# A state-space layer and a gated feed-forward on one core: the head without a diagonal, up rows loaded ahead of x tile 2, and its transposes in two banks

## The chip, the cores and the metric

The kernel runs on one core of one Trainium2 chip. The metric is the device time of one launch in microseconds (us); of several runs the median is taken. A core has five engines, each with a queue of its own that it works off in order: TensorE (PE in the profile; PEld is its weight load), VectorE (DVE), ScalarE (ACT), GpSimd (POOL) and SyncE (SP, which here only issues transfers). They wait for each other through semaphores. TensorE writes only to PSUM, which has eight banks of 128 x 512 float32; VectorE and ScalarE copy the results out ("evict" them) to SBUF.

## The reference

Input x is 2048 x 512 in bfloat16. It is normalised by rows, and two branches work on the result:

```python
x = A_x
xn = layernorm(x)                                  # rows of 512
# A: a diagonal complex state-space layer, 512 states
Lam_bar = exp(exp(log_dt) * Lam)
Bu = xn @ B_bar.T
h[t] = Lam_bar * h[t-1] + Bu[t]                    # 2048 steps
A = 2 * real(h @ C.T) + xn * Dskip
# B: a gated feed-forward, 512 -> 1376 -> 512
B = (silu(xn @ w_gate) * (xn @ w_up)) @ w_down
out = x + A + B                                    # bfloat16
```

## The kernel before

The 2048 rows are 16 tiles of 128 rows, in four chunks of four tiles. Every engine's instructions stand in an order written out by hand. Later chunks are normalised, transposed by DMA into xnT and multiplied from there. Chunk 0 has its own way through gate and up, so that TensorE can start before any row is normalised: this is the head, and the change is in it.

**Head, tiles 0 and 1.** The column sum of each row tile is not taken off in SBUF but in PSUM. TensorE transposes the raw tile in four blocks of 128 columns by products with the identity (`raw_mm`, `cT_mm`, L244) and adds a product of the constant minus_mean (all entries -1/512) with a diagonal matrix of the row sums (`cT_mean`, L252). The sums come from VectorE for tile 0 (`sum_dve`, L221) and from ScalarE for tile 1 (`sum_act`, L224); `diag_dve` (L231) makes the diagonals. `cT_copy` (L256) copies each block, centred and transposed, into xcT. Warming products (`dummy`, L646) on a constant go ahead of and between these.

**Head, tiles 2 and 3.** Tile 2 is centred in SBUF with a mean from ScalarE (`mean_act`, L227; `center`, L234), tile 3 with the mean of its statistics. TensorE then transposes the centred tile into one bank (p1 for tile 2, p0 for tile 3) and ScalarE copies it out whole.

**Gate and up of chunk 0.** `head_mm` (`sw_mm`, L488) multiplies the transposed blocks with the first 512 columns of w_gate (which = 0) and w_up (which = 1); their 512 rows come in four row blocks k of 128, as weights wg and wu. Results of tile i stay in the banks held[i][0] and held[i][1] until `sw_out` (L497, L498) evicts them on ScalarE with a factor rstd, the row's inverse deviation. rstd needs statistics (`ln_stats`, L187 and L188, on VectorE), a variance plus eps (`ln_rstd`, L196, VectorE) and a power on GpSimd (L197). After the head two more groups of columns follow in the same way for all four tiles (gi = 1, 2), with new banks: group 1's third gate tile gets the bank that held[2][0] had.

**Beside it.** On GpSimd, behind the rstd powers, `exp_pool` (L284) makes dt_t, then come the memsets of `pad_last`, an iota (L725) and another power. On VectorE, behind the head, come `norm_dve` (L205), which writes the normalised tiles for the transpose by DMA, and the small parameter steps `params_a` and `params_sin` (L287 to L334). The two sines of `params_sin` (L339, L341) stand in ScalarE's queue between sw_out of tile 1 and sw_out of tile 2.

**Loads.** SP's queue loads, in this order: x tile 0, w_gate row blocks 0 and 2, x tile 2, w_up row blocks 0 and 1 together, 2 and 3 together, x tile 3, and the later groups. ScalarE's queue loads x tile 1 and w_gate row blocks 1 and 3.

Of the kernel before, what the change touches and what calls it, by code (L numbers as in the profile page):

```python
# [10 lines left out]
F32 = mybir.dt.float32  # L11
BF16 = mybir.dt.bfloat16
ALU = mybir.AluOpType
ACT = mybir.ActivationFunctionType
# [9 lines left out]
def kernel(  # L24
# [17 lines left out]
    nc = tc.nc  # L42
    _, L, D = A_x.shape
# [4 lines left out]
    HW = CW // 2  # L48
    NT = L // 128
    NCH = L // CW  # L50
    TPC = CW // 128
    KD = D // 128
# [11 lines left out]
    const = ctx.enter_context(tc.tile_pool(name="const", bufs=1))  # L64
# [9 lines left out]
    def bank(shape=(128, CW), dtype=F32):  # L74
        return psum.tile(list(shape), dtype, name="ps")

    def flat(ap3):
        return ap3.rearrange("p q j -> p (q j)")
# [4 lines left out]
    wu_v = B_w_up.rearrange("(k p) f -> p k f", p=128)  # L83


    xall = const.tile([128, NT, D], BF16, name="xall")
    xnT = const.tile([128, NCH, KD, CW], BF16, name="xnT")

    fgroups = [(0, 4), (4, 8), (8, FT - 1)]
    wg_g, wu_g = [], []  # L90
# [26 lines left out]
    def load_w1_half(q, tiles, view, gi, k0, k1):  # L117
        a, b = fgroups[gi]
        q.dma_start(out=tiles[gi][:, k0:k1, :], in_=view[:, k0:k1, a * 128:min(F, b * 128)])

    HK = KD // 2
    ident = const.tile([128, 128], BF16, name="ident")
    make_identity(nc, ident[:])
    minus_mean = const.tile([128, 128], BF16, name="minus_mean")
    nc.sync.dma_start(out=xall[:, 0, :], in_=x_v[:, 0, :])
    nc.vector.memset(xall[:, 1, 0:2], 0.0)
    nc.vector.memset(minus_mean[:], -1.0 / D)
    nc.scalar.dma_start(out=xall[:, 1, :], in_=x_v[:, 1, :])
    nc.scalar.preload_act_table_set("silu_and_others")
    for k in range(KD):  # L130
        load_w1_half(nc.scalar if k % 2 else nc.sync, wg_g, wg_v, 0, k, k + 1)
    nc.sync.dma_start(out=xall[:, 2, :], in_=x_v[:, 2, :])
    load_w1_half(nc.sync, wu_g, wu_v, 0, 0, HK)
    load_w1_half(nc.sync, wu_g, wu_v, 0, HK, KD)
    nc.sync.dma_start(out=xall[:, 3, :], in_=x_v[:, 3, :])
    load_w1(nc.sync, wg_g, wg_v, 1)
# [35 lines left out]
    mv = const.tile([128, NT, 2], F32, name="mv")  # L172
# [10 lines left out]
    def by_k(ap):  # L183
        return ap.rearrange("p (k d) -> p k d", d=128)

    def ln_stats(n):
        nc.vector.bn_stats(out=stats[:, n, 0, :], in_=xall[:, n, :])  # L187
        nc.vector.bn_aggr(out=mv[:, n, :], in_=stats[:, n, 0, :])  # L188

    def ln_stats_half(n, h):  # L190
        nc.vector.bn_stats(out=stats[:, n, h, :], in_=xall[:, n, h * HW:(h + 1) * HW])
        if h == 1:
            nc.vector.bn_aggr(out=mv[:, n, :], in_=stats[:, n, :, :])

    def ln_rstd(a, b):
        nc.vector.tensor_scalar(out=ve[:, a:b], in0=mv[:, a:b, 1], scalar1=EPS, scalar2=None, op0=ALU.add)  # L196
        nc.gpsimd.tensor_tensor(out=rstd[:, a:b], in0=ve[:, a:b], in1=neg_half[:, 0:b - a], op=ALU.pow)  # L197
# [16 lines left out]

    xcT, xc = CF[:, 0], CF[:, 1]
    xn_c[0] = flat(xc).rearrange("p (k i d) -> p k i d", k=KD, i=TPC)
    sums = const.tile([128, 2], F32, name="sums")
    diag = const.tile([128, 2, 128], BF16, name="diag")

    def sum_dve(i):  # L220
        nc.vector.tensor_reduce(out=sums[:, i:i + 1], in_=xall[:, i, :], axis=mybir.AxisListType.X, op=ALU.add)  # L221

    def sum_act(i):
        nc.scalar.activation(out=xnT[:, NCH - 1, 0, :], in_=xall[:, i, :], func=ACT.Copy, accum_out=sums[:, i:i + 1])  # L224

    def mean_act(i):
        nc.scalar.activation(out=xnT[:, NCH - 1, 0, :], in_=xall[:, i, :], func=ACT.Copy, scale=1.0 / D,  # L227
                             accum_out=mean2[:])

    def diag_dve(i):  # L230
        nc.vector.tensor_scalar(out=diag[:, i, :], in0=ident[:], scalar1=sums[:, i:i + 1], scalar2=None, op0=ALU.mult)  # L231

    def center(i, mean):
        nc.vector.tensor_scalar(out=xc[:, i, :], in0=xall[:, i, :], scalar1=mean, scalar2=None, op0=ALU.subtract)  # L234

    mean2 = const.tile([128, 1], F32, name="mean2")
    p2, p0, p1 = bank(), bank(), bank()
    held = [[None, None] for _ in range(TPC)]
    held[0][0], held[1][0], held[0][1], held[1][1], held[2][0] = (bank() for _ in range(5))
    warm = held[1][0]  # L240
    raw = [[p0, p1, held[2][0], held[1][1]], [p2, p2, held[0][1], held[0][1]]]

    def cT_mm(ps, src, k, first, stop):
        nc.tensor.matmul(ps[:, k * 128:(k + 1) * 128], lhsT=src[:, k * 128:(k + 1) * 128], rhs=ident[:], start=first,  # L244
                         stop=stop)

    def raw_mm(i):
        for k in range(KD):
            cT_mm(raw[i][k], xall[:, i, :], k, k == 0 or raw[i][k] is not raw[i][k - 1], False)

    def cT_mean(i, k0, k1):
        nc.tensor.matmul(raw[i][k0][:, k0 * 128:k1 * 128], lhsT=minus_mean[:],  # L252
                         rhs=diag[:, i:i + 1, :].to_broadcast([128, k1 - k0, 128]), start=False, stop=True)

    def cT_copy(copy, ps, i, k0=0, k1=KD):
        copy(out=xcT[:, k0:k1, i * 128:(i + 1) * 128], in_=by_k(ps[:, k0 * 128:k1 * 128]))  # L256

    seen = const.tile([128, 1], BF16, name="seen")

    def runs(ap):  # L260
        return ap.rearrange("p k (i t) -> p (k i) t", t=128)
# [14 lines left out]
    V = nc.vector  # L276
# [208 lines left out]
    def sw_mm(ps, groups, gi, i, k0=0, k1=KD):  # L485
        a, b = fgroups[gi]
        for k in range(k0, k1):
            nc.tensor.matmul(ps[:, 0:(b - a) * 128], lhsT=xcT[:, k, i * 128:(i + 1) * 128], rhs=groups[gi][:, k, 0:(b - a) * 128],  # L488
                             start=(k == 0), stop=(k == KD - 1))
# [154 lines left out]
    def dummy(ps, n, cols):  # L644
        for _ in range(n):
            nc.tensor.matmul(ps[:, 0:cols], lhsT=one.to_broadcast([128, 128]), rhs=one.to_broadcast([128, cols]),  # L646
                             start=True, stop=True)
# [22 lines left out]
    def head_mm(which, i, k0=0, k1=KD):  # L670
        if held[i][which] is None:
            held[i][which] = bank()
        sw_mm(held[i][which], (G, U)[which], 0, i, k0, k1)

    dummy(warm, 4, CW)
    dummy(warm, 5, 128)
    V.tensor_copy(out=seen[:], in_=ident[:, 0:1])
    sum_dve(0)
    sum_act(1)
    diag_dve(0)  # L680
    raw_mm(0)
    raw_mm(1)
    dummy(warm, 2, 128)
    for k in range(KD):
        cT_mean(0, k, k + 1)
    diag_dve(1)
    for k in range(KD):
        cT_copy(nc.scalar.copy if k % 2 else V.tensor_copy, raw[0][k], 0, k, k + 1)
    cT_mean(1, 0, HK)
    head_mm(0, 0, 0, 1)  # L690
    cT_mean(1, HK, KD)
    cT_copy(V.tensor_copy, raw[1][0], 1, 0, HK)
    cT_copy(nc.scalar.copy, raw[1][HK], 1, HK, KD)
    head_mm(0, 0, 1, HK)
    head_mm(0, 1, 0, HK)
    for k in range(HK, KD):
        for i in range(2):
            head_mm(0, i, k, k + 1)
    ln_stats(1)
    mean_act(2)  # L700
    ln_rstd(1, 2)
    ln_stats_half(0, 0)
    center(2, mean2[:])
    ln_stats_half(0, 1)
    ln_rstd(0, 1)
    for i in range(2):
        head_mm(1, i, 0, HK)
    for k in range(KD):
        cT_mm(p1, xc[:, 2, :], k, k == 0, k == KD - 1)
    cT_copy(nc.scalar.copy, p1, 2)  # L710
    for i in range(2):
        head_mm(1, i, HK, KD)
    ln_stats(3)
    center(3, mv[:, 3, 0:1])
    ln_rstd(3, 4)
    ln_stats(2)
    ln_rstd(2, 3)
    head_mm(0, 2)
    for k in range(KD):
        cT_mm(p0, xc[:, 3, :], k, k == 0, k == KD - 1)  # L720
# [158 lines left out]
```

## Time and profile before

| | us |
|---|---|
| median of three runs | 178.81 |
| lowest and highest | 178.35, 178.82 |
| profiled execution, its own time | 178.46 |
| its span, first to last instruction | 176.4 |
| TensorE busy in the span | 172.9 (98%) |
| VectorE busy | 158.1 (90%) |
| ScalarE busy | 106.6 (60%) |
| GpSimd busy | 27.8 (16%) |

The profile is of one execution. Times in the timeline are counted from the start of the span; each line gives start, busy time, engine, line of the kernel, operation, what it writes and reads, the number of instructions, and in brackets the idle time before it and what ended it. Matmuls are pipelined, so the busy time of a group is longer than the distance to the next group's start: the distance between starts tells the pace. The page gives the granted clock of TensorE as full throughout; the rows in the first microseconds are slower than later ones of the same form.

Landings of the loads, from the trace (us): x tile 0 3.20, x tile 1 3.54, w_gate rows 0 to 3 3.91, 4.28, 5.47 and 6.02, x tile 2 6.42, w_up rows 0 and 1 6.94, rows 2 and 3 7.62, x tile 3 8.00.

### The profile page before, as it was taken

The numbers are of one execution on the slowest core, as the hardware profiler recorded it, in microseconds if no ns is written. First come the engines' busy times: TensorE is split into PE (matmuls) and PEld (weight loads), VectorE is DVE, ScalarE is ACT, GpSimd is POOL, SyncE is SP. The second block draws the span as 40 slices with busy tenths as digits, with TensorE's granted clock in tenths as the row PEclk, the third lists the DMA queues.
The fourth block names the chain that finished last, engine by engine and source line by source line (L and its number), as shares of the span: only waits on it lengthen the run. The fifth ranks groups of instructions, "written<-read, shape, count | busy, mean of one in ns | idle before, by whom it ended". The sixth has DMA issues, their size and how long they took to land.

```text
span 176.4 us, 2469 instructions
## 1 busy us (share of the span) xinstructions
PE 172.9 (98%) x904; PEld 85.4 (48%) x904; DVE 158.1 (90%) x261; ACT 106.6 (60%) x192; POOL 27.8 (16%) x39
## 2 busy tenths in 40 slices
PE   8999999999999999999999999999999999999993
PEld 4444755564444444446444444446444444444743
DVE  3899999999999999999999999999999997799133
ACT  4468989978976687036896661024666657962000
POOL 5272300050000000047000000024100002416100
PEclk9999999999999999999999999999999999999999
DMA  6999839999996000037015000007410000993712
GB/s 169 340 351 203 177 88 250 224 169 337 238 238 238 4 0 0 0 33 85 16 20 119 0 0 0 0 4 71 48 30 2 4 0 0 160 181 48 90 44 75
DMA packets 35179, 17.88 MB, mean 101 GB/s; under 512 B 25008, under 2 KB 35088, under 8 KB 35120
## 3 DMA queue, kind: packets, MB, share of 16 engines
q1 hardware_dynamic: 30992, 13.96, 33.8%
q0 software_dynamic: 3456, 3.28, 14.6%
q10 hardware_dynamic: 720, 0.49, 0.9%
q8 instruction: 7, 0.11, 0.3%
q14 instruction: 4, 0.03, 0.1%
HBM read 8.03 MB, written 5.24 MB: 75 GB/s over the span
## 4 chain that ended last, share of the span: by engine, by line
PE 97%; DMA 1%; DVE 0%; issue 0%
PE ps L461 29%; PE ps L579 22%; PE ps L589 16%; PE ps L386 16%; PE ps L488 10%; PE ps L521 3%; DMA xall<-in_A_x_dram 1%; PE ps L244 1%; PE ps L252 0%; DVE xall L592 0%; PE ps L646 0%; PE ps L280 0%
## 5 line engine op out<-in xcount | busy, mean ns | idle before, releaser
L579 PE MATMUL ps<-wd_sb,guT 128*128 128x512 bf16 (+3 forms) x198 | 38.8, 355 | 0.0
L428 DVE TENSOR_TENSOR_SCAN g<-r_t,car,u 128x512 bf16<-128x512 f32 x24 | 29.1, 1264 | 0.0
L589 PE MATMUL ps<-CF,wt 128*128 128x512 bf16 (+2 forms) x144 | 28.3, 355 | 0.0
L386 PE MATMUL ps<-xnT,BT 128*128 128x512 bf16 x128 | 28.3, 379 | 0.0
L579 PEld LDWEIGHTS <-guT 128*128 128x128 bf16 (+1 forms) x198 | 18.5, 98 | 19.9
L461 PE MATMUL ps<-xnT,wg 128*128 128x512 bf16 x96 | 24.6, 379 | 0.0
L461 PE MATMUL ps<-xnT,wu 128*128 128x512 bf16 x96 | 24.6, 379 | 0.0
L596 POOL DMA_DIRECT2D out_dram<-res x12 | 10.5, 1043 | 81.6 <-ACT res L595 76.0
L595 ACT CAST res<-ps 128x512 bf16<-128x512 f32 x12 | 7.0, 584 | 24.7 <-PE ps L589 24.7
L388 ACT CAST u<-ps 128x512 bf16<-128x512 f32 x32 | 18.2, 590 | 5.9 <-PE ps L386 5.8
L475 ACT ACTIVATE guT<-ps 128x512 bf16<-128x512 f32 x30 | 17.9, 596 | 6.1 <-PE ps L461 6.1
L476 ACT CAST u<-ps 128x512 bf16<-128x512 f32 x30 | 17.6, 587 | 6.0 <-PE ps L461 6.0
L589 PEld LDWEIGHTS <-wt 128*128 128x128 bf16 x144 | 13.4, 98 | 14.3
L386 PEld LDWEIGHTS <-BT 128*128 128x128 bf16 x128 | 12.5, 98 | 14.7
L551 ACT ACTIVATE xr<-xall,nb,rstd 128x512 bf16<-128x512 bf16 x16 | 11.8, 804 | 5.2 <-DVE xall L559 3.0
L461 PEld LDWEIGHTS <-wu 128*128 128x128 bf16 x96 | 9.4, 98 | 11.3
L461 PEld LDWEIGHTS <-wg 128*128 128x128 bf16 x96 | 9.4, 98 | 10.6
L488 PEld LDWEIGHTS <-CF 128*128 128x128 bf16 x96 | 9.1, 98 | 8.0 <-ACT CF L256 0.8
L197 POOL TENSOR_TENSOR rstd<-ve,neg_half 128x1 f32<-128x1 f32 (+1 forms) x7 | 7.6, 1084 | 26.7 <-DVE ve L196 26.7
L461 PE MATMUL ps<-xnT,w_end 128*128 128x512 bf16 x48 | 10.8, 379 | 0.0
L187 DVE BATCH_NORM_STATS2 stats<-xall 128x6 f32<-128x512 bf16 x15 | 10.1, 674 | 0.2 <-DMA xall<-in_A_x_dram 0.2
L480 DVE TENSOR_TENSOR guT<-guT,u 128x1024 bf16<-128x1024 bf16 x15 | 10.0, 675 | 0.0
(120 smaller groups left out, 217.9 us busy)
## 6 DMA issues: line engine op xcount, KB each, us to landing
out_dram<-in_A_x_dram SPq DMA_DIRECT2D x3, 512.0 KB, 5.2
out_dram<-res POOLq DMA_DIRECT2D x12, 128.0 KB, 3.1
out_dram<-xall POOLq DMA_DIRECT2D x3, 512.0 KB, 6.1
wd_sb<-in_B_w_down_dram SPq DMA_DIRECT2D x1, 1280.0 KB, 7.2
xall<-in_A_x_dram SPq DMA_DIRECT2D x1, 1024.0 KB, 7.3
wu<-in_B_w_up_dram SPq DMA_DIRECT2D x2, 256.0 KB, 4.4
wg<-in_B_w_gate_dram SPq DMA_DIRECT2D x1, 512.0 KB, 5.3
wu<-in_B_w_up_dram SPq DMA_DIRECT2D x1, 512.0 KB, 5.4
```

The source lines that it names most:

```text
L187: nc.vector.bn_stats(out=stats[:, n, 0, :], in_=xall[:, n, :])
L386: nc.tensor.matmul(ps[:], lhsT=BT[:, part, k, q * 128:(q + 1) * 128], rhs=xnT[:, c, k, :], start=(k == 0), stop=(k == KD - 1))
L388: nc.scalar.copy(out=u_tiles[c][:, part, q, :], in_=ps[:])
L428: V.tensor_tensor_scan(out=g()[:, part, q, :], data0=r_t[:, q:q + 1].to_broadcast([128, CW]), data1=u_tiles[c][:, part, q, :], initial=ini ...
L461: nc.tensor.matmul(ps[:fs, lo:hi], lhsT=wslice(groups, fi, k), rhs=xnT[:, c, k, lo:hi], start=(k == 0), stop=(k == KD - 1))
L475: nc.scalar.activation(out=guT[:fs, fi, :], in_=psg[:fs], func=ACT.Silu)
L476: nc.scalar.copy(out=u_pair[c][:fs, fi % 2, :], in_=psu[:fs])
L488: nc.tensor.matmul(ps[:, 0:(b - a) * 128], lhsT=xcT[:, k, i * 128:(i + 1) * 128], rhs=groups[gi][:, k, 0:(b - a) * 128], start=(k == 0), s ...
L551: nc.scalar.activation(out=box["xr"][:], in_=xall[:, n, :], func=ACT.Identity, scale=rstd[:, n:n + 1], bias=nb[:, n:n + 1])
L579: nc.tensor.matmul(o[:], lhsT=gu_tiles[c][:fsz[fi], fi, i * 128:(i + 1) * 128], rhs=wd_sb[:fsz[fi], fi, lo:hi], start=(fi == 0), stop=False)
L589: nc.tensor.matmul(o[:], lhsT=w_tiles[c][:, part, q, i * 128:(i + 1) * 128], rhs=CF[:, part, q, lo:hi], start=False, stop=(part == 1 and q ...
L596: nc.gpsimd.dma_start(out=out_v[:, n, lo:hi], in_=res[:, lo:hi], accum_op=ALU.add)
```

## The change

- The diagonals are gone. The row sums (now bfloat16) are used as weights, each column repeated 128 times, against a constant diagonal of -1/512: minus_mean is now the identity times -1/512, made on VectorE.
- Both sums come from VectorE: one pass that adds the two halves of a row (256 columns each) and accumulates the total. ScalarE sums nothing any more.
- The order of transposes, mean products and copies of tiles 0 and 1 is new. Copies of even blocks are on ScalarE, of odd blocks on VectorE. Tile 1's blocks 0 and 2 share a bank, and 1 and 3, with one mean product for each bank; these two stand behind the first gate product. The two warming products between transposes and means are gone.
- w_up rows 0 and 1 are loaded ahead of x tile 2.
- Tile 2 is transposed after row blocks 0 to 2 of up and ahead of row block 3, into two banks: p1, copied by ScalarE, and p0, copied by VectorE.
- The means of tiles 2 and 3 come from the new sum pass and a small scaling on VectorE. The statistics of tiles 1, 2 and 3 stand on VectorE behind the centring of tile 3, and rstd of tiles 2 and 3 is one operation.

```diff
-    nc.vector.memset(minus_mean[:], -1.0 / D)
...
+    load_w1_half(nc.sync, wu_g, wu_v, 0, 0, HK)
     nc.sync.dma_start(out=xall[:, 2, :], in_=x_v[:, 2, :])
-    load_w1_half(nc.sync, wu_g, wu_v, 0, 0, HK)
     load_w1_half(nc.sync, wu_g, wu_v, 0, HK, KD)
...
+    def sum_dve(i, dst):
+        nc.vector.scalar_tensor_tensor(out=xnT[:, NCH - 1, i, 0:HW], in0=xall[:, i, 0:HW], scalar=1.0,
+                                       in1=xall[:, i, HW:D], op0=ALU.mult, op1=ALU.add, accum_out=dst)
+
+    def center(i):
+        total, m = mean[:, i - 2, 0:1], mean[:, i - 2, 1:2]
+        sum_dve(i, total)
+        nc.vector.tensor_scalar(out=m, in0=total, scalar1=1.0 / D, scalar2=None, op0=ALU.mult)
+        nc.vector.tensor_scalar(out=xc[:, i, :], in0=xall[:, i, :], scalar1=m, scalar2=None, op0=ALU.subtract)
...
-    raw = [[p0, p1, held[2][0], held[1][1]], [p2, p2, held[0][1], held[0][1]]]
+    raw = [[p0, p1, held[2][0], held[1][1]], [p2, held[0][1], p2, held[0][1]]]
...
-    def cT_mean(i, k0, k1):
-        nc.tensor.matmul(raw[i][k0][:, k0 * 128:k1 * 128], lhsT=minus_mean[:],
-                         rhs=diag[:, i:i + 1, :].to_broadcast([128, k1 - k0, 128]), start=False, stop=True)
+    def cT_mean(i, *ks):
+        nc.tensor.matmul(by_k(raw[i][ks[0]][:])[:, ks[0]:ks[-1] + 1:HK], lhsT=sums[:, i:i + 1].to_broadcast([128, 128]),
+                         rhs=minus_mean[:, None, :].to_broadcast([128, len(ks), 128]), start=False, stop=True)
+
+    def raw_copy(i, k):
+        cT_copy(V.tensor_copy if k % 2 else nc.scalar.copy, raw[i][k], i, k, k + 1)
...
-    V.tensor_copy(out=seen[:], in_=ident[:, 0:1])
-    sum_dve(0)
-    sum_act(1)
-    diag_dve(0)
+    nc.vector.tensor_scalar(out=minus_mean[:], in0=ident[:], scalar1=-1.0 / D, scalar2=None, op0=ALU.mult)
+    for i in range(2):
+        sum_dve(i, sums[:, i:i + 1])
     raw_mm(0)
+    for k in range(HK):
+        cT_mean(0, k)
+        raw_copy(0, k)
     raw_mm(1)
-    dummy(warm, 2, 128)
-    for k in range(KD):
-        cT_mean(0, k, k + 1)
-    diag_dve(1)
-    for k in range(KD):
-        cT_copy(nc.scalar.copy if k % 2 else V.tensor_copy, raw[0][k], 0, k, k + 1)
-    cT_mean(1, 0, HK)
+    for k in range(HK, KD):
+        cT_mean(0, k)
     head_mm(0, 0, 0, 1)
-    cT_mean(1, HK, KD)
-    cT_copy(V.tensor_copy, raw[1][0], 1, 0, HK)
-    cT_copy(nc.scalar.copy, raw[1][HK], 1, HK, KD)
+    for k in range(HK):
+        cT_mean(1, k, k + HK)
+        raw_copy(1, k)
     head_mm(0, 0, 1, HK)
+    for k in range(HK, KD):
+        raw_copy(0, k)
     head_mm(0, 1, 0, HK)
+    for k in range(HK, KD):
+        raw_copy(1, k)
     for k in range(HK, KD):
         for i in range(2):
             head_mm(0, i, k, k + 1)
+    ln_stats(0)
+    ln_rstd(0, 1)
+    center(2)
+    for k in range(KD - 1):
+        for i in range(2):
+            head_mm(1, i, k, k + 1)
+    for h, (ps, copy) in enumerate(((p1, nc.scalar.copy), (p0, V.tensor_copy))):
+        for k in range(h * HK, (h + 1) * HK):
+            cT_mm(ps, xc[:, 2, :], k, k % HK == 0, k % HK == HK - 1)
+        cT_copy(copy, ps, 2, h * HK, (h + 1) * HK)
+    for i in range(2):
+        head_mm(1, i, KD - 1, KD)
+    center(3)
     ln_stats(1)
-    mean_act(2)
     ln_rstd(1, 2)
-    ln_stats_half(0, 0)
-    center(2, mean2[:])
-    ln_stats_half(0, 1)
-    ln_rstd(0, 1)
-    for i in range(2):
-        head_mm(1, i, 0, HK)
-    for k in range(KD):
-        cT_mm(p1, xc[:, 2, :], k, k == 0, k == KD - 1)
-    cT_copy(nc.scalar.copy, p1, 2)
-    for i in range(2):
-        head_mm(1, i, HK, KD)
+    ln_stats(2)
     ln_stats(3)
-    center(3, mv[:, 3, 0:1])
-    ln_rstd(3, 4)
-    ln_stats(2)
-    ln_rstd(2, 3)
+    ln_rstd(2, 4)
     head_mm(0, 2)
```

More of the change, by code (lines that the diff above doesn't have):

```diff
@@ L216 @@
     xn_c[0] = flat(xc).rearrange("p (k i d) -> p k i d", k=KD, i=TPC)
[L217 to L236, printed above, removed]
+    sums = const.tile([128, 2], BF16, name="sums")
+    mean = const.tile([128, 2, 2], F32, name="mean")
+    def sum_dve(i, dst):
[6 more added lines that the diff above has]
+        nc.vector.tensor_scalar(out=xc[:, i, :], in0=xall[:, i, :], scalar1=m, scalar2=None, op0=ALU.subtract)
     p2, p0, p1 = bank(), bank(), bank()
@@ L248, in raw_mm @@
         for k in range(KD):
-            cT_mm(raw[i][k], xall[:, i, :], k, k == 0 or raw[i][k] is not raw[i][k - 1], False)
-    def cT_mean(i, k0, k1):
-        nc.tensor.matmul(raw[i][k0][:, k0 * 128:k1 * 128], lhsT=minus_mean[:],
-                         rhs=diag[:, i:i + 1, :].to_broadcast([128, k1 - k0, 128]), start=False, stop=True)
+            cT_mm(raw[i][k], xall[:, i, :], k, all(p is not raw[i][k] for p in raw[i][:k]), False)
+    def cT_mean(i, *ks):
[3 more added lines that the diff above has]
+        cT_copy(V.tensor_copy if k % 2 else nc.scalar.copy, raw[i][k], i, k, k + 1)
     def cT_copy(copy, ps, i, k0=0, k1=KD):
         copy(out=xcT[:, k0:k1, i * 128:(i + 1) * 128], in_=by_k(ps[:, k0 * 128:k1 * 128]))
-    seen = const.tile([128, 1], BF16, name="seen")
     def runs(ap):
```

## The prediction

> **What bounds the kernel now.** I read the chain of waits first, then the timeline of the first 26 us engine by engine, then the landings of the loads.
>
> ```profile
> ## 4 chain that ended last, share of the span: by engine, by line
> PE 97%; DMA 1%; DVE 0%; issue 0%
> ```
>
> TensorE is the chain from 3.25 us to the end, so an edit counts only by what it adds to or takes from TensorE's queue. TensorE in the head (start, busy, engine, line):
>
> ```profile
> 3.25 1.03 PE L244 MATMUL ps<-ident,xall 128*128 128x128 bf16 x8
> 4.08 0.42 PE L646 MATMUL ps<-const-bfloat16-1.0 128*128 128x128 bf16 x2
> 4.29 0.85 PE L252 MATMUL ps<-diag,minus_mean 128*128 128x128 bf16 x5
> 4.99 0.51 PE L488 MATMUL ps<-wg,CF 128*128 128x512 bf16 x1
> ...
> 5.45 1.68 PE L488 MATMUL ps<-wg,CF 128*128 128x512 bf16 x7
> 6.98 1.02 PE L488 MATMUL ps<-wu,CF 128*128 128x512 bf16 x4
> ...
> 9.79 0.39 PE L244 MATMUL ps<-ident,CF 128*128 128x128 bf16 x4
> ...
> 16.11 1.03 PE L488 MATMUL ps<-wg,CF 128*128 128x512 bf16 x4
> ```
>
> Two rates show. Up to about 5.27 us a 128-column product follows the last after 107 ns and a 512-column one would take 0.427 us; afterwards it is 56 ns and 0.216 us (four in 0.86 us). From 5.45 us TensorE never waits measurably; the first up product sits at 6.98 because up rows 0 and 1 land at 6.94, but it was due at 5.45 + 7 x 0.216 = 6.96. The last line, group 1's third gate tile, matters below. The other engines:
>
> ```profile
> 3.23 0.69 DVE L221 TENSOR_REDUCE sums<-xall 128x1 f32<-128x512 bf16 x1 [1.72 <-DMA xall<-in_A_x_dram]
> ...
> 6.52 0.42 DVE L191 BATCH_NORM_STATS2 stats<-xall 128x6 f32<-128x256 bf16 x1
> ...
> 10.51 0.15 DVE L196 TENSOR_SCALAR ve<-mv 128x1 f32<-128x1 f32 x1
> 10.59 0.17 DVE L281 COPY prm<-ps 128x12 f32<-128x12 f32 x1
> ...
> 12.79 0.48 DVE L334 TENSOR_SCALAR kk<-ws 128x8 f32<-128x8 f32 x1
> ```
> ```profile
> 10.74 0.69 POOL L197 TENSOR_TENSOR rstd<-ve,neg_half 128x1 f32<-128x1 f32 x1 [0.45 <-DVE ve L196]
> 11.26 1.02 POOL L284 TENSOR_TENSOR dt_t<-e_t,prm 128x4 f32<-128x4 f32 x1
> ```
> ```profile
> 13.50 0.21 ACT L339 ACTIVATE sin<-fs 128x8 f32<-128x8 f32 x1 [0.38 <-DVE fs L325]
> 13.99 0.21 ACT L341 ACTIVATE cos<-fc 128x8 f32<-128x8 f32 x1 [0.28 <-DVE fc L325]
> 14.10 0.67 ACT L497 ACTIVATE guT<-ps,rstd 128x512 bf16<-128x512 f32 x1
> ```
>
> This second chain hangs on VectorE: the last variance (10.66), its rstd on GpSimd, the exponential dt_t behind it in GpSimd's queue, small parameter steps on VectorE, sin and cos on ScalarE, and only then, in ScalarE's queue, the eviction of tile 2's gate (14.10 to 14.77). Its bank, held[2][0], is the one that group 1's third gate tile takes at 16.11, in both kernels. Margin: 1.34 us. The change spends it.
>
> **The change, part by part (new times).**
>
> *Sums instead of diagonal.* Before: 0.69 reduce, then a 0.25 diagonal, ready at 4.20. Now one two-input pass over 256 columns with a running sum, which no row shows. Below: a two-input bf16 pass of 1024 takes 0.68, so 256 by its slope over a floor of 0.15 give 0.28. Above: 0.69, the reduce of 512. I take 0.42, the 256-column row above, as nearest. Sum 0 is ready at 3.65, 0.55 earlier. The repeated column as weights costs nothing extra (the warming products load such weights at the same pace). minus_mean is made at 1.35 in VectorE's wait for x tile 0.
>
> *Order of TensorE.* Four transposes from 3.25, then at the slow rate eight small products from 3.71 to 4.56. The first gate product goes at 4.56 (4.99 before; its copy is done at 4.33, its weights landed at 3.91), but still slow, so it ends at 4.99. Only behind it come tile 1's two mean products (256 columns each; before, one of them ran ahead of the gate, at 4.72). The first starts at 4.99, is in the bank 0.42 later, and its copy on ScalarE takes 0.27: 5.45 to 5.72. The second gate product runs at 5.35; tile 1's first can go only at 5.78 (5.66 before), after a wait of 0.21. Six products at 0.216 lead to the first up product at 7.07 instead of 6.98: **+0.09**. The two 107 ns warming products that are dropped and the 0.43 at the start are lost again here.
>
> *Loads.* Rows 0, 1 of up (256 KB) now precede x tile 2 (128 KB). In 6.02 to 8.00 us the queue landed 768 KB, about 0.35 us per 128 KB, so up lands at about 6.6 and x tile 2 at about 6.95 instead of 6.42; later ones stay. Up is not needed before 7.07, so its advance hides. x tile 2 is needed at 7.22, when VectorE has finished tile 0's statistics; cover 0.27 us, beyond which each 0.1 costs up to 0.1.
>
> *x tile 2.* VectorE: sum 0.42, scale 0.15, centre 0.35 with 0.03 between, from 7.22 to 8.22. TensorE does six up products to 8.37, so they are just hidden. Transposes to 8.59, up's last row to 9.02. ScalarE's half copy (0.37) runs 8.68 to 9.05; the next gate product waits for it until 9.11: **+0.09**. VectorE's half is not needed before 9.54.
>
> *x tile 3.* Its centring now waits behind the half copy (8.81 to 9.24) and makes its own sum: 9.16 + 0.42 + 0.15 + 0.35 and gaps give 10.15. TensorE arrives at 9.97 and starts at 10.21: **+0.23**. Transposes at 10.21 instead of 9.79, 0.42 late in all.
>
> *Statistics.* Before, those of tiles 1, 0 and 3 lay in VectorE's gaps and only tile 2's came after tile 3's centring. Now tiles 1, 2 and 3 come after it: each 0.69 + 0.18 and gaps, two variance steps of 0.15, from 10.07 to 13.02 (10.66 before). GpSimd's rstd for two columns lies between 0.56 (one) and 1.02 (a power of four); 0.75 gives 13.10 to 13.85. dt_t follows in that queue and ends at 14.83 (12.28 before). Then the same steps as before, 12.28 to 14.10, that is 1.82: tile 2's gate eviction goes at 16.65 and frees its bank at 17.32. Behind sin and cos ScalarE's whole queue waits, about 2.9 us instead of 0.7. TensorE reaches the bank at 16.11 + 0.42 = 16.53 and starts at 17.38: **+0.85**.
>
> In that 1.82 lies the 0.48 of kk (L334); the same operation takes 0.17 at 13.58. It ended at 13.26, when GpSimd's iota ended at 13.24. That order follows dt_t in both kernels, so I keep it; without it the sum would be 0.30 less. [...]
>
> *Afterwards.* ScalarE evicts every 0.57 us (11.28 to 11.85), TensorE fills a bank in 0.86, so ScalarE regains ground; in group 2 (0.36 against 0.43) the smallest margin is still 0.14. VectorE runs 2.3 us late. The normalised tile 0..3 is ready at 14.63 instead of 12.21, but SP's queue issued its transpose only at 14.43, so this costs 0.3; it lands at about 20.9 and is needed at 24.3.
>
> **Sum.** 0.09 + 0.09 + 0.23 + 0.85 = 1.26 us, on the profiled execution's 178.46 (span 176.4 and 2.1 around it): 179.7. The median shown is 178.81, 0.35 above that execution; 178.81 + 1.26 = 180.1. I take 179.9 between them.
>
> **Rivals.**
>
> *Faster.* The early start survives. Gate row 3 lands at 6.02, so gate could end at 6.5 and up start at 6.6, 0.35 early: 178.1 to 178.5. That needs tile 1's copies done by 5.56, tile 3 centred by 9.4, and tile 2's gate evicted by 15.7. For it: sum 0 really comes 0.55 earlier. Against it: three waits, each from rows that repeat. 0.04.
>
> *Only the head slips.* If the bank were free by 16.5, 0.41 would remain: 178.9 to 179.2, partly no change. It needs 0.85 out of VectorE's and GpSimd's chain; the shortest values for sum and rstd together save 0.33. 0.06.
>
> *Slow sums or late x tile 2.* With 0.69 for each sum the mean products start at 4.0, x tile 2 and 3 wait longer, and the total is 1.8; x tile 2 landing at 7.7 gives 1.7: 180.2 to 180.6. 0.17.
>
> *The fast rate comes later.* The rate changed 4.5 us after the first product. [...] 0.03. [...]
>
> **How the numbers follow.** The forecast itself has 0.70. Its bounds: 0.28 for the sums and 0.58 for rstd give +0.93, on the lowest run (178.35) 179.3; slow sums on the median give 180.6. I set 179.2 to 180.8. A measurement here tells about 0.3% (0.54 us) from no change. Faster 0.04; same 0.05, most of the head-only case; slower 0.91.
>
> **What would show it.** In the changed kernel: first gate product near 4.6 but first up product near 7.1; tile 3's transposes near 10.2; dt_t ending near 14.8; sin near 16.0; a TensorE wait of about 0.85 at group 1's third gate tile, ended by ScalarE's eviction. It is wrong if TensorE does not wait there, or if dt_t ends before 14 us.

## The result, and the profile after

The changed kernel takes 180.03 us (median of 6 runs, 179.75 to 180.44); the kernel before takes 178.86 in the same measurement (6 runs, 178.35 to 179.27). The ratio is 1.0074, with a 95% interval from 1.0056 to 1.0091: slower by 1.2 us. The profiled execution of the changed kernel took 180.06 (span 178.0), that of before 178.46 (span 176.4). So the two traces differ by 1.6 us and the medians by 1.17: before's trace is of one of its quicker executions, after's of a middling one.

The chain that ended last, as the page of the changed kernel gives it, is no longer TensorE from the head to the end:

```profile
## 4 chain that ended last, share of the span: by engine, by line
PE 69%; DVE 19%; ACT 4%; DMA 4%; issue 1%; POOL 1%; DVEq 0%
```

VectorE's 19% must not be read as "VectorE is now the bound". The view of what each engine waits for shows only one wait of TensorE after the head:

```profile
engine line waited for: us in total, times, longest us
PE ps L639 <- PEq L856: 0.8, 1, 0.8
PE ps L481 <- ACT guT L490: 0.6, 1, 0.6
```

The first line is in the kernel before too, under its own line numbers. The second is the forecast one. The chain follows VectorE on to 44.8 us and comes back to TensorE at 53.12 through evictions that ended just in time: the distance there, 52.26 to 53.12 for four products, is the undisturbed 0.86. TensorE's lines in the timeline of the changed kernel (start, busy, engine, line; L481 is the old L488, L236 the old L244):

```profile
4.44 0.63 PE L481 MATMUL ps<-wg,CF 128*128 128x512 bf16 x1
4.87 0.63 PE L244 MATMUL ps<-minus_mean,sums 128*128 128x256 bf16 x2
5.30 1.96 PE L481 MATMUL ps<-wg,CF 128*128 128x512 bf16 x7
7.09 1.75 PE L481 MATMUL ps<-wu,CF 128*128 128x512 bf16 x6
8.68 0.38 PE L236 MATMUL ps<-ident,CF 128*128 128x128 bf16 x4
...
9.42 1.04 PE L481 MATMUL ps<-wg,CF 128*128 128x512 bf16 x4
10.57 0.40 PE L236 MATMUL ps<-ident,CF 128*128 128x128 bf16 x4
```

Gate starts at 4.44 instead of 4.99, and nothing of it is left at the first up product: 7.09 against 6.98. Tile 3's transposes are 0.78 late (10.57 against 9.79), and group 1's third gate tile is 1.53 late (16.11 before):

```profile
17.64 0.59 PE L481 MATMUL ps<-wg,CF 128*128 128x512 bf16 x2 [0.57 <-ACT guT L490]
```

The last product of the kernel is late by the same 1.53 (175.02 against 173.49), so the loss is complete at this line. Half of it came in the head (0.78), half at the bank (0.75). The second chain, engine by engine, in the same timeline:

```profile
13.17 0.17 DVE L195 TENSOR_SCALAR ve<-mv 128x2 f32<-128x2 f32 x1
...
15.60 0.47 DVE L327 TENSOR_SCALAR kk<-ws 128x8 f32<-128x8 f32 x1
```
```profile
13.42 0.70 POOL L196 TENSOR_TENSOR rstd<-ve,neg_half 128x2 f32<-128x2 f32 x1 [1.25 <-DVE prm L274]
14.08 1.01 POOL L277 TENSOR_TENSOR dt_t<-e_t,prm 128x4 f32<-128x4 f32 x1
...
15.50 0.56 POOL L718 IOTA jidx<- 128x512 f32 x1
```
```profile
16.31 0.21 ACT L332 ACTIVATE sin<-fs 128x8 f32<-128x8 f32 x1 [2.40 <-DVE fs L318]
16.80 0.21 ACT L334 ACTIVATE cos<-fc 128x8 f32<-128x8 f32 x1 [0.28 <-DVE fc L318]
16.92 0.67 ACT L490 ACTIVATE guT<-ps,rstd 128x512 bf16<-128x512 f32 x1
```

The bracket of sin is the line to see: ScalarE stands idle for 2.40 us before it, behind an instruction whose input VectorE has not made, while tile 2's gate has been ready for eviction since about 14.1, when its rstd was done. It is evicted 16.92 to 17.59, and TensorE goes on at 17.64.

### The profile page after: what moved, and what is told of

It is laid out like the page before. It is cut to its first block, busy times and chain, and to the rows that moved or that the text cites. A ratio compares the mean times of both kernels' runs of the same rounds, so it can differ in the third digit from the quotient of the medians.

```text
span 178.0 us, 2451 instructions
## 1 busy us (share of the span) xinstructions
PE 172.8 (97%) x886; PEld 85.3 (48%) x902; DVE 159.0 (89%) x267; ACT 103.8 (58%) x189; POOL 27.6 (15%) x38
## 4 chain that ended last, share of the span: by engine, by line
PE 69%; DVE 19%; ACT 4%; DMA 4%; issue 1%; POOL 1%; DVEq 0%
PE ps L454 22%; PE ps L572 21%; PE ps L582 15%; PE ps L379 8%; DVE stats L186 4%; DMA wu<-in_B_w_up_dram 3%; DVE pm L302 3%; DVE pm L389 2%; ACT guT L468 2%; DVE guT L495 2%; DVE pm L301 2%; PE ps L514 1%; DMA xall<-in_A_x_dram 1%; ACT xn L209 1%; ACT u L469 1%
## 5 line engine op out<-in xcount | busy, mean ns | idle before, releaser
L572 PE MATMUL ps<-wd_sb,guT 128*128 128x512 bf16 (+4 forms) x197 | 38.7, 355 | 0.1
L481 PEld LDWEIGHTS <-CF 128*128 128x128 bf16 x96 | 9.2, 99 | 9.0 <-ACT CF L251 1.3
L196 POOL TENSOR_TENSOR rstd<-ve,neg_half 128x4 f32<-128x4 f32 (+2 forms) x6 | 7.1, 1176 | 30.6 <-DVE ve L195 29.3
L186 DVE BATCH_NORM_STATS2 stats<-xall 128x6 f32<-128x512 bf16 x16 | 10.8, 673 | 0.0
```

The source lines that it names most:

```text
L572: nc.tensor.matmul(o[:], lhsT=gu_tiles[c][:fsz[fi], fi, i * 128:(i + 1) * 128], rhs=wd_sb[:fsz[fi], fi, lo:hi], start=(fi == 0), stop=False)
```

## The experiments

The theory after the result: the loss sits in ScalarE's queue, where sin and cos, waiting for a parameter chain that VectorE now starts later, stand ahead of tile 2's gate eviction. The rivals: the exchanged loads, or the head alone, make the loss. All kernels below were timed against the kernel before on the same chips, whose medians there were 178.72 to 178.79; the changed kernel itself (180.03, against 178.86) was not timed again, so the ratios to before compare best. The sums and the order of TensorE are as changed unless said.

**The sines out of the way.** From the changed kernel; only ScalarE's order changes.

```diff
 def params_sin():
     ...
-        nc.scalar.activation(out=sin1[:], ..., func=ACT.Sin, ...)
-        nc.scalar.activation(out=cos1[:], ..., func=ACT.Sin, ...)
+def params_sines():          # called right behind sw_out(0, 3, ...)
+        nc.scalar.activation(out=sin1[:], ..., func=ACT.Sin, ...)
+        nc.scalar.activation(out=cos1[:], ..., func=ACT.Sin, ...)
```

> The changed kernel, with the two small sines of params_sin moved in ScalarE's queue from ahead of tile 2's evictions to behind tile 3's; nothing else. Theory (the wait at tile 2's gate bank is made by sin and cos, which wait for dt_t): tile 2's gate eviction no longer waits for dt_t, only for rstd of tile 2 (ready at about 14.1), so it goes at about 14.2 instead of 16.9; TensorE does not wait at group 1's third gate tile, and the kernel gains the 0.75 to 0.85 us of that wait: about 179.2. Rival (the loss lies in the loads or in the late fast rate): TensorE's wait there is not what costs, time stays at about 180.0.

Measured: 179.29 (12 runs), ratio to before 1.0032 [1.0018, 1.0046], against 1.0074 for the change: 0.74 us came back, the bank's half of the loss. ScalarE and TensorE in the timeline of this kernel:

```profile
14.27 0.69 ACT L492 ACTIVATE guT<-ps,rstd 128x512 bf16<-128x512 f32 x1 [0.23 <-POOL rstd L196]
...
16.57 0.23 ACT L335 ACTIVATE sin<-fs 128x8 f32<-128x8 f32 x1
```
```profile
17.03 1.03 PE L483 MATMUL ps<-wg,CF 128*128 128x512 bf16 x4
```

Tile 2's gate leaves 2.65 us earlier, as soon as its rstd is there, and TensorE passes the bank without a wait. (TensorE comes to it at 17.03 here; in this execution it waited 0.36 in the head for w_gate's row block 2, which landed at 6.44; more on that below.)

**Tile 1's statistics earlier.** From the changed kernel; VectorE alone changes, which shortens the chain by one tile's statistics instead of taking it out of ScalarE's way.

```diff
     center(2)
+    ln_stats(1)
+    ln_rstd(1, 2)
     for k in range(KD - 1):
     ...
     center(3)
-    ln_stats(1)
-    ln_rstd(1, 2)
     ln_stats(2)
```

> The changed kernel with the statistics of tile 1 moved on VectorE from behind tile 3's centring to between tile 2's centring and tile 2's half copy, where VectorE idles 0.7 us. Theory (dt_t is late because the statistics stand behind the centring): dt_t ends about 0.7 earlier; the half copy and tile 3's centring go about 0.3 later, so tile 3's transposes slip by 0.3 while the bank is free 0.7 earlier: the time falls by 0.6 to 0.7, to about 179.4. Rival (VectorE's order does not matter, GpSimd or ScalarE alone is late): tile 3's slip costs 0.3: 180.3.

Measured: 179.40 (12 runs), 1.0035 [1.0020, 1.0049]. dt_t starts at 13.57 instead of 14.08, the eviction at 16.40, and TensorE has no wait at the bank, which it reaches at 17.40. That is late in part because this execution, the slowest of the twelve (179.82), waited 0.85 for w_gate's row block 2 in the head. What the edit itself pays is in the head too, in the timeline of this kernel:

```profile
11.07 0.40 PE L236 MATMUL ps<-ident,CF 128*128 128x128 bf16 x4 [0.31 <-DVE CF L227]
```

**Tile 3's centring ahead of tile 2's half copy.** From the changed kernel, again VectorE alone.

```diff
     center(2)
+    center(3)
     for k in range(KD - 1):
     ...
-    center(3)
     ln_stats(1)
```

> The changed kernel with tile 3's sum, mean and centring ahead of tile 2's half copy on VectorE. Theory: tile 3's transposes no longer wait (0.2 to 0.3 at 10.5), the statistics start about 0.7 earlier and with them dt_t and tile 2's eviction; TensorE still waits at the bank, so the gain is that of the bank, about 0.7: 179.3. Rival (the wait at tile 3's transposes adds to the end by itself, the bank's wait does not): gain 0.3: 179.7.

Measured: 179.16 (12 runs), 1.0022 [1.0010, 1.0034]. Tile 3's transposes go at 10.48 without a wait of their own (the four gate products ahead of them take 0.17 longer; VectorE's half copy now comes behind the centring), dt_t at 13.55, and the gate eviction at 16.38 leaves 0.3 us of the bank's wait (TensorE is due at 16.8 and starts at 17.10). So three edits that share nothing but this chain, one on ScalarE and two on VectorE, each take away more than half of the wait, and 0.63 to 0.87 us of the time (0.70 to 0.93 by the ratios). The two traces on VectorE are not clean, for TensorE waited 0.85 and 0.61 in their heads for w_gate's row block 2; the edit of the sines leaves the statistics and dt_t as late as they were and still frees the bank. With the control below, I count the wait at the bank as shown.

**The loads put back.** From the changed kernel, with x tile 2 ahead of up's rows 0 and 1 as in the kernel before.

```diff
-    load_w1_half(nc.sync, wu_g, wu_v, 0, 0, HK)
     nc.sync.dma_start(out=xall[:, 2, :], in_=x_v[:, 2, :])
+    load_w1_half(nc.sync, wu_g, wu_v, 0, 0, HK)
```

> The changed kernel with the load order of before (x tile 2 ahead of up rows 0 and 1). Theory (the order of the loads matters little): x tile 2 lands about 0.5 us earlier and up rows 0, 1 about 0.4 later; the first up product may start up to 0.3 later, at the landing, but up's third row block then waits less; the total moves by less than 0.2: 179.9 to 180.2. Rival (the swap itself delays the rows behind it: rows 2 and 3 landed at 8.21 in the changed kernel's profile against 7.62 before): rows 2, 3 land at 7.6 to 7.7 again and 0.3 is gained: 179.7.

Measured: 179.95 (6 runs), 1.0073 [1.0050, 1.0095]: no difference from the change that this can tell, though some tenths could hide in the interval. The bank's wait stays, in the timeline:

```profile
7.00 1.46 PE L481 MATMUL ps<-wu,CF 128*128 128x512 bf16 x6
...
17.25 1.02 PE L481 MATMUL ps<-wg,CF 128*128 128x512 bf16 x4 [0.56 <-ACT guT L490]
```

**The exchange of loads alone**, put into the kernel before; the diff is the last one the other way round.

> The kernel before with only the exchange of loads: up rows 0 and 1 ahead of x tile 2. Theory of the prediction (x tile 2 lands 0.5 later, all else as before): ScalarE's mean and the centring of tile 2 come 0.5 later, tile 2's transposes wait about 0.3 to 0.4 at 7.84; margin at tile 2's gate bank falls from 1.34 to about 1, no wait there: 179.1. Rival (the new order also delays w_gate row block 2 and all behind it by 0.7 to 1.0): two waits, in the gate products and at tile 2's transposes: 0.7 or more, 179.5 and up.

Measured: 179.22 (12 runs), 1.0025 [1.0015, 1.0036], so 0.5 us slower. TensorE's one wait in the head of this kernel:

```profile
8.32 0.40 PE L244 MATMUL ps<-ident,CF 128*128 128x128 bf16 x4 [0.35 <-DVE CF L234]
```

These transposes of tile 2 went at 7.84 before; x tile 2 landed at 7.07 instead of 6.42. So the exchange has a price of its own, which the changed kernel does not show in full: there the second chain's wait comes last and the head's delay partly lies beside it.

**The sines moved in the kernel before**, as a control: there the eviction at 14.10 has 1.34 us to spare, so moving it should bring nothing.

> Control: the kernel before with the two sines moved behind tile 3's evictions, as in the first experiment. Theory (the sines cost only where dt_t comes late; here tile 2's gate bank is free 1.3 us before TensorE asks for it): no change, 178.6 to 178.8. Rival (the move is worth 0.7 us by itself, whatever the head does): 178.0.

Measured: 178.48 (12 runs), 0.9987 [0.9972, 1.0002]. The interval still holds no change; a gain of the 0.7 that the same edit gave in the changed kernel is excluded.

**Both the sines and tile 3's centring**, from the changed kernel: do their gains add up?

> The changed kernel with both edits: the two sines behind tile 3's evictions, and tile 3's centring ahead of tile 2's half copy. Theory (after the bank's wait only the waits of the head are left, and the one at tile 3's transposes adds to the end once the bank does not wait): 0.2 to 0.3 below the sines alone (179.29), so 179.0, within 0.3 of the kernel before. Rival (the two gains are the same one, both act through dt_t): no better than the better of the two alone, 179.2 to 179.3.

Measured: 179.18 (12 runs), 1.0019 [1.0006, 1.0032]. The median lies with the rival, that each alone already takes most of the same loss (179.29 and 179.16 alone). But the interval, 178.83 to 179.29, holds my 179.0 as well, and five of the twelve runs lie at 178.84 or below. The profiled execution, one of these five, has no wait of TensorE at the bank, which it reaches at 16.48. Whether the gains add up stays open.

**Also tile 1's mean products ahead of the first gate product**, from the last kernel:

```diff
-    head_mm(0, 0, 0, 1)
     for k in range(HK):
         cT_mean(1, k, k + HK)
         raw_copy(1, k)
+    head_mm(0, 0, 0, 1)
     head_mm(0, 0, 1, HK)
```

> As the run with both edits, and tile 1's two mean products ahead of the first gate product on TensorE. Theory of the head's first wait (tile 1's copies come 0.1 to 0.2 late because its means stand behind a gate product at the slow rate): 0.1 to 0.2 less than the run with both edits, about 178.85, where w_gate row block 2 has landed early enough. Rival (w_gate row block 2, landing at 6.2 to 6.7 in the profiles with the new load order, sets when the gate goes on): no gain, 179.0.

Measured: 178.88 (12 runs), 1.0010 [0.9997, 1.0022]. The step to the kernel without this edit is 0.3, and the two intervals overlap: it is not shown to be more than noise. Gate then runs as one row of eight in the timeline, without a gap between its products:

```profile
4.89 2.66 PE L483 MATMUL ps<-wg,CF 128*128 128x512 bf16 x8
7.38 1.46 PE L483 MATMUL ps<-wu,CF 128*128 128x512 bf16 x6
```

Eight products at 0.216 would take 1.73; these take 2.49, which is what some 3.6 products at the slow 0.427 and the others at 0.216 give, and the record of the full clock begins at 6.43 us in this execution. Here the early start gave little.

**And the old order of loads on top of that.**

> As the run with the means ahead, and with the load order of before. Rival of the loads (the new order makes w_gate row block 2 land about 1 us later, 6.2 to 6.7 against 5.2 to 5.5 in the profiles with the old order, and this costs once nothing hides it): 0.2 to 0.4 less than the run with the means ahead, 178.5 to 178.6. Theory of the prediction (the order only exchanges x tile 2 and the up rows): no difference beyond 0.1.

Measured: 178.75 (12 runs), 1.0001 [0.9987, 1.0016]. The difference of 0.13 lies between what the two theories expected and inside the noise; this run settles nothing on the loads. Its trace shows what an early start meets next: gate starts at 4.28, already at the fast rate (its first four products are busy for 1.15 us in all; at the slow rate their starts alone would lie 1.28 apart), and then waits 0.62 for w_gate's row block 2, which lands at 6.01.

**A version meant to win**: the last kernel, with tile 2 centred first of all, its transposes after four up products, and tile 3's centring back behind the half copy.

```diff
+    center(2)
     ln_stats(0)
     ln_rstd(0, 1)
-    center(2)
-    for k in range(KD - 1):
+    for k in range(HK):
         for i in range(2):
             head_mm(1, i, k, k + 1)
     ...                                  # tile 2's transposes, copies
-    for i in range(2):
-        head_mm(1, i, KD - 1, KD)
+    for k in range(HK, KD):
+        for i in range(2):
+            head_mm(1, i, k, k + 1)
     center(3)
```

> The sums as weights with all waits of the head taken out as far as the runs showed them: load order of before, tile 1's mean products ahead of the first gate product, tile 2's centring ahead of tile 0's statistics, tile 2's transposes after two row blocks of up (four products cover its copies), tile 3's centring behind tile 2's half copy, the two sines behind tile 3's evictions. Theory: what is left over the kernel before is the earlier start of the gate products, some 0.2 us of TensorE work done by 5.3 us: 178.5 to 178.7, at most 0.1% faster. Rival (the landings of w_gate row block 2 and of up rows 0 and 1 bind, not the sums): no difference from before, 178.7 to 178.8.

Measured: 178.61 (12 runs), 0.9991 [0.9977, 1.0005]: not told from the kernel before. TensorE in its timeline:

```profile
4.68 2.19 PE L483 MATMUL ps<-wg,CF 128*128 128x512 bf16 x8
6.93 1.02 PE L483 MATMUL ps<-wu,CF 128*128 128x512 bf16 x4
7.79 0.39 PE L236 MATMUL ps<-ident,CF 128*128 128x128 bf16 x4
...
16.06 1.03 PE L483 MATMUL ps<-wg,CF 128*128 128x512 bf16 x4
```

Gate starts 0.31 earlier than before and its last product goes at 6.49 (4.68 + 2.19, less the 0.38 of one product), so up was due at 6.71; up's first rows land at 6.89, so up starts at 6.93. From there on each line is 0.05 ahead of the kernel before. In this trace the loads of up take back what the sums without a diagonal save.

**The kernel before, profiled once more:**

> The kernel before once more, for a second profile of its loads and of the moment at which TensorE's rate doubles. Theory of the load order (the old order lands w_gate row block 2 earlier): 5.2 to 6.0, and up's second half at 7.3 to 7.8, as in the three profiles with that order. Rival (landings only vary between executions): anywhere from 5.2 to 6.7.

Measured: 178.76 in the profiled execution. w_gate's row block 2 lands at 6.00, at the end of the expected range, and up's second half at 7.98, outside it. x tile 2 lands at 6.70 and up's first rows at 7.21, and the first up product goes at 7.26, where the trace that I predicted from has 6.42, 6.94 and 6.98. So 0.28 of time in the head comes and goes between executions of one kernel, and the trace that was shown first is the quicker of the two.

## Why the prediction was right

The forecast was 179.9 and the measurement 180.03. By its steps:

- **Sums.** The pass of 256 columns takes 0.42, as chosen between 0.28 and 0.69. A second record follows each, in VectorE's timeline of the changed kernel:

```profile
3.12 0.42 DVE L220 SCALAR_TENSOR_TENSOR xnT<-xall 128x256 bf16<-128x256 bf16 x1 [1.57 <-DMA xall<-in_A_x_dram]
3.47 0.09 DVE L220 DVE_READ_ACCUMULATOR xnT<-xall 128x1 bf16 x1
3.54 0.43 DVE L220 SCALAR_TENSOR_TENSOR xnT<-xall 128x256 bf16<-128x256 bf16 x1
```

  Two sums therefore start 0.42 apart, and the slow-sum rival falls.
- **Order of TensorE.** First up product at 7.09, forecast 7.07. The +0.09 is +0.11.
- **Loads: the step that was wrong.** I put up's rows 0 and 1 at 6.6, x tile 2 at 6.95 (the pace that I read off, 0.33 to 0.35 per 128 KB from 6.02, gives 6.7 and 7.0 to 7.1) and left the later ones where they were. They landed at 7.01, 7.43, and up's rows 2 and 3 at 8.21 instead of 7.62. So VectorE waited 0.22 for x tile 2, and TensorE, due at up's third row block at about 7.96, started it at 8.25: 0.29 that no step held. That makes the head's loss 0.78 where the steps gave 0.42. TensorE's own delay does not reach the end, for TensorE then waits at the bank anyway; what reaches it is that VectorE's chain is 0.27 later. In the trace with the loads put back the steps come out nearly as I had them: tile 3's transposes at 10.18 (forecast 10.21), dt_t's end at 14.71 (14.83), the eviction at 16.53 (16.65), TensorE at the bank at 17.25 (17.38). That is one execution, the quickest of its six; the medians of the two orders (179.95 and 180.03) do not show such a gain.
- **x tile 2's half copy.** TensorE waited 0.08 there, forecast 0.09; at 9.42 instead of 9.11.
- **Tile 3's centring.** TensorE waited 0.28, forecast 0.23; at 10.57 instead of 10.21.
- **Statistics and GpSimd.** The last variance ends at 13.34 (13.02 forecast, and 0.32 late for the reasons above), the power of two columns takes 0.70 (0.75), dt_t ends at 15.09 (14.83).
- **From dt_t to the eviction.** 15.09 to 16.92 is 1.83, forecast 1.82, the slow kk with it: 0.47, and it ends at 16.07, when the iota ends at 16.06. The 0.30 that the slow kk adds thus came as forecast, and as in the trace before, where the two end at 13.26 and 13.24. Not every operation of VectorE beside GpSimd's was slow here: the second kk (16.39) took 0.17 beside the power r_t, and the four steps of norm_dve took 0.40 to 0.42 each beside the powers rstd and dt_t, and the next four 0.40 to 0.41 with GpSimd idle (24.7 to 26.7). Since kk and the iota both follow dt_t in every run, none of them tests whether the iota is what slows kk.
- **The bank.** TensorE stood still for 0.73 by the distance of starts (16.69 to 17.64, less one product of 0.22), which the profile's bracket gives as 0.57. Forecast 0.85. With the later head, both ends of this wait moved: TensorE came later by 0.38, the eviction by 0.27.

The sum of 1.26 against 1.53 in the traces is short by those 0.27, which is how late VectorE's chain was in this trace; against the medians it is 0.09 too much. The difference of the two I can only lay to the executions: the loads vary between them, and before's trace has them early. That 179.9 came within 0.13 of 180.03 is therefore in part luck, for its base was a choice between two values 0.35 apart. The mechanism and the place of the loss are not luck. Of the rivals, the one of the head alone needed a free bank by 16.5, and TensorE waited there until 17.64. That of the late x tile 2 came half true, without its price. The one of the fast rate did not happen: the full rate begins at 5.50 here and at 5.28 before (how this is read, below); what would put it off, no run shows.

What stays open: how much of the changed kernel's 1.2 us, and of the 0.5 that is left without the bank's wait, is due to the exchanged loads. Alone they cost 0.5; put back in the changed kernel, they gave 0.08 with intervals of 0.3 to 0.4 to each side. And three edits gave back 0.63 to 0.87 each of a loss of 1.2, so the parts have no sum.

## What to carry to other kernels

When a step is taken out ahead of the bound engine, look at what the next input is (here up's weights at 6.9 us) before counting the time as saved, and at what other queues were reordered to make room. An instruction that waits on a long side chain, as the two tiny sines did, held up everything behind it in its queue here (ScalarE stood idle for 2.40 us, and moving the sines gave 0.74 us): put it behind the evictions that free banks, not ahead of them. Cost every late chain from its own first late operation to the buffer that it holds, and compare it with when that buffer is needed; that margin (1.34 us here) is what an edit elsewhere may spend.

## What was not expected of the hardware

**A load landed later when a larger one stood next behind it in the queue.** w_gate's row block 2 stands in SP's queue ahead of the two loads that were exchanged, so its place did not change. Yet it landed at 5.18 to 6.01 us in six traces with the old order, and at 5.89 to 6.70 in seven with the new one; up's rows 2 and 3, behind both, at 7.28 to 7.98 and 7.87 to 8.47, with the same bytes ahead of them. The windows of the profile from 3.25 to 5.60 us (length, busy time of TensorE, its weight load, VectorE, ScalarE and GpSimd, granted clock, busy share of the DMA engines, GB/s), first before, then after:

```profile
3.25:5.60 2.35, 2.35 (x18) 1.68 (x18) 2.10 (x7) 1.20 (x4) 0.30 (x1) 1.00 1.06 317
```
```profile
3.25:5.60 2.35, 2.35 (x16) 1.51 (x15) 1.07 (x6) 0.54 (x3) 0.30 (x1) 1.00 0.95 216
```

The transfer engines are nearly as busy (0.95 against 1.06), and move a third less (216 against 317 GB/s). This pair is an extreme one: over all thirteen traces the same window has 235 to 317 GB/s with the old order and 216 to 266 with the new, and the second profile of the kernel before has 235. So the throughput does not tell the orders apart. The landings of row block 2 overlap only at their ends and lie 0.6 apart in the mean (5.67 and 6.30); what delays them was not found.

**The moment at which TensorE gets fast varies much, and the clock column does not show it.** Eleven of the thirteen traces hold a record of TensorE's full clock. It begins at 3.83 us at the earliest and 6.43 at the latest, though the first warming product is always at 0.78, and the distance of the products halves there (in the kernel before the record begins at 5.28: 107 ns for 128 columns ahead of it and 56 behind it). For the time ahead the traces hold no record, and the views count time without one as 1.00, as in the windows above. So the full clock that the page gives throughout says nothing of the first microseconds: there the distance of the products decides. What sets the moment, and why it moves by 2.6 us, was not found. The heads of these kernels differ somewhat; the two traces of the kernel before have 5.28 and 5.64. At half the rate those 0.36 us are 0.18 us of TensorE's work, by my estimate, which can be a part of the difference between single executions of the same kernel (178.17 to 179.52 for the kernel before), and it is a reason to compare medians of several runs, and traces only where both are past that point.
